# A fused attention and two-layer expert kernel: first-batch attention outputs copied to SBUF, and a new order of all steps

## The chip, the cores and the metric

The kernel runs on one core of a Trainium2 chip. The time is the device time of one execution in microseconds, the median of three runs. The engines are TensorE (PE; its weight loads are shown apart as PEld), VectorE (DVE), ScalarE (ACT), GpSimd (POOL) and SyncE (SP), which sends all the DMA transfers of this kernel from one queue, in order. Each engine works off its own instructions in order.

## The reference

Three stages follow each other; everything is float32, and the inputs of stage 2 and 3 have 1152 rows.

```python
# stage 1: attention, 2 batches x 8 heads x 576 positions x 64
rel = pos[:, None] - pos[None, :]
mask_plain = (rel >= 0) & (rel < 32)                    # heads 0 to 3
mask_dil = (rel >= 0) & (rel < 128) & (rel % 4 == 0)    # heads 4 to 7
scores = np.where(masks, (q @ k.T) / 8, -1e9)
attn = softmax(scores);  x = (attn @ v) -> 1152 x 512
# stage 2: w_in 512 x 1024, w_out 1024 x 512
h = x @ w_in
solu = h * softmax(h)
ln = (solu - mean) / sqrt(var + 1e-6) * g_ln
x = ln @ w_out
# stage 3: 4 experts, w1 512 x 1024, w2 1024 x 512 each
p = domain_probs / domain_probs.sum(-1)
out = sum over e of p[:, e] * (relu(x @ w1[e]) @ w2[e])
```

## The kernel before

Every matrix product outside the attention is computed from split operands: a value is held as a high part in a short form and a low part (value minus high part), and a product is three matmuls, high x high, high x low and low x high. `w_in` and `w_out` come as 64-bit floats and are rebuilt to float32 and split on the chip.

**Stage 1.** Per batch there are six units of attention: `UP.t.b` for the plain heads, `UD.t.b` for the dilated ones (t = 0 to 2, b the batch). A unit (`att_U`) starts with the masks (L264, L268) and the scores (L277) on PE into a PSUM tile `pa`, of which there are two buffers. DVE takes the maximum (L285) and subtracts it (L287); ACT does the exponential (L290); DVE sums (L292) and inverts (L294); the weights `pd` are multiplied on DVE or POOL (L296). PE transposes them (L315) into a `pa`, they are copied to `pt` (L170, L172), and PE multiplies with V (L326, the AV product) into another `pa`. The last two steps write the split output: the high part `xhi` by a copy from PSUM (ACT L172 or DVE L170), the low part `xlo` by `lo_psum` (L246), a subtraction on DVE of the high part in SBUF from the PSUM tile. Units in `ASWAP` are transposed by DVE and a round trip through DRAM instead (`sta`, `da`, L301 to L309).

**The weights.** `VI.j` rebuilds and splits block j of `w_in` (`VI.4` is the second half of block 0) in seven steps: two passes of ACT (L186, L188), a shift (L190) and a merge (L192) on DVE, an addition (L194), the high part `wh` (L170, L172), and the low part `wl` (L221). `VO.j.t` does that for `w_out` (`conv_out`, low part L237); its raw data is in `cvr`, of which there are two halves. `l...` are loads, by SyncE: `lP`, `lD` for the scores' inputs `qkP`, `qkD`, `lvp`, `lvd` for V, `lI` for `w_in` (`draw`), `lO` for `w_out`.

**Stage 2.** `H.t` (`moe_H`, L356) multiplies token tile t of 128 rows with `w_in`: four quarters, of six matmuls each, one for each block of `w_in`, then the reductions of the gated softmax and of the normalization. `T.t` transposes the result, on PE for tiles 0 to 2 and through DRAM for the others, and splits it into `hh` and `hl`. `X.c.dp` (`moe_X`, L432) multiplies chunk c of three token tiles with `w_out`.

**Stage 3.** Each expert's two layers, 512 x 1024 and 1024 x 512, are computed with seven products of quarter matrices in place of eight, `u` (L545) and `d` (L617). `XQ`, `WP` and `WV` prepare the sums of operands for it.

**What sets the order.** Everything up to the middle of the first expert is issued by the table `ORDER`, L27 to L50. Each step is a Python generator, and one name in the table runs it to its next `yield`. A `+` behind a name sets `alt[0]` for this step: a `copy` then runs on DVE instead of ACT (`copy`, L168), and a `pick()` on POOL instead of DVE (L162). `F.n` issues n matmuls on a constant tile whose output nobody reads. The table decides the order on every engine and in SyncE's queue, since nothing else reorders.

Of the kernel before, what the change touches and what calls it, by code (L numbers as in the profile page):

```python
# [26 lines left out]
ORDER = """  # L27
lP.0.0+ F.6 UP.0.0 UP.0.0+ lI.0 UP.0.0 lD.0.0 VI.0 VI.0 VI.0+ VI.0 F.6 UD.0.0 UP.0.0 UP.0.0+ lI.4 VI.0 VI.4+ UD.0.0 UP.0.0+ VI.4 UD.0.0+ UD.0.0+ lD.1.0+ VI.4
VI.4 VI.4+ lP.1.0+ F.3 UD.1.0 UD.1.0 UD.1.0+ UD.0.0 UD.0.0 UD.1.0+ UP.1.0 UP.1.0 UD.1.0 UD.1.0+ UP.0.0 VI.0 UP.1.0+ lD.2.0+ F.1 UD.2.0+ UD.2.0 lP.2.0 F.1
UP.2.0 UD.0.0+ UD.2.0 VI.4 UP.1.0+ UP.1.0+ lI.1+ UP.1.0+ VI.1+ VI.1+ UD.1.0+ lvd.1.0+ UP.2.0 UP.2.0+ UP.2.0 UD.1.0 VI.1+ VI.1 F.3 UP.0.0 UP.1.0 UD.1.0 VI.4+  # L30
F.1 UD.1.0+ UD.1.0+ UP.0.0 lI.2+ UD.1.0+ VI.0+ lvp.0.0+ UP.0.0 VI.2+ VI.2 UP.0.0 UP.0.0+ VI.1+ F.3 H.0+ VI.2 VI.2+ UD.2.0 VI.1 VI.1 UD.0.0 UD.0.0 UP.2.0+
UP.1.0 lI.3 UP.1.0 lvd.0.0 UD.0.0+ lvp.1.0 UP.1.0 lvp.2.0+ H.0+ UD.2.0+ VI.3 UD.0.0 UD.0.0 UP.1.0 UP.1.0 VI.3+ UD.2.0 VI.3 lP.0.1 UP.0.1 H.1 H.1 VI.2+ VI.2
UP.0.1 UP.0.1+ UP.0.1+ lO.0.0+ VO.0.0 VI.3 UD.2.0+ UD.2.0 UD.2.0 VI.3 VI.3 VI.3+ VI.2 lD.0.1+ UD.0.1 UD.0.1 UD.0.1+ lvp.0.1 lD.1.1+ UP.0.1 UP.2.0+ lvd.2.0+
UD.1.1 VO.0.0 lO.0.1 VO.0.1 UP.0.1 H.0 UD.1.1 VO.0.0 UD.2.0 UD.2.0 VO.0.0 VO.0.0+ H.0 UP.2.0+ lO.1.0+ lD.2.1 UD.2.0 H.0+ UD.0.1 UD.0.1+ endE+ UD.1.1+ VO.0.1+
VO.0.1+ H.0+ H.0 H.1 H.1 misc+ UP.0.1+ UP.0.1 UD.0.1+ UD.0.1+ H.1+ UP.2.0 UD.1.1 UD.0.1+ UD.0.1 UP.0.1 UP.0.1 UP.2.0 H.0+ UP.0.1 UP.0.1+ VO.0.1+ UD.1.1
lvd.1.1 UP.2.0 VO.0.1+ H.2 UP.2.0 lvd.0.1+ UP.2.0 UD.1.1 H.1+ H.1+ UD.1.1+ VO.0.0+ VO.0.0+ VO.0.1+ VO.0.1+ UD.2.1 UD.2.1+ VO.1.0+ VO.1.0 VO.1.0+ VO.1.0 lP.2.1
VO.1.0+ T.0 H.1+ lvp.2.1+ UD.2.1 lO.1.1+ UD.0.1+ T.0+ T.0 H.2+ UD.1.1+ UD.1.1+ H.2 UD.2.1+ UD.2.1+ T.0+ UD.2.1 UD.2.1+ T.1+ T.1 T.1 H.3 T.1 H.2 H.2 lP.1.1
VO.1.1+ VO.1.1 VO.1.1+ lO.2.0+ UD.0.1+ UD.0.1 UP.2.1+ UP.2.1+ UD.0.1+ VO.1.0 VO.1.0 VO.1.1 UD.1.1+ UP.2.1+ H.2+ UD.2.1+ UD.2.1 H.3 H.3 VO.2.0 VO.2.0 VO.1.1+
lO.2.1 UP.2.1 UD.1.1+ UP.2.1+ lvd.2.1 UD.1.1 T.2 VO.2.0+ UD.1.1+ H.4 T.2+ T.2 UD.2.1 VO.1.1+ UP.2.1 VO.2.0 VO.2.0+ lO.3.0+ T.2 H.3+ H.3+ UP.2.1+ UP.2.1 VO.1.1
H.4 UP.1.1 VO.2.1 VO.2.1 VO.2.1+ UP.2.1 UP.1.1 UP.2.1 VO.2.1+ VO.2.1+ lO.3.1 lvp.1.1 H.4+ H.4+ UP.1.1 H.3+ VO.2.0 VO.2.0 X.0.1 UP.1.1+ VO.3.0+ UP.1.1 UP.1.1+  # L40
UP.1.1 UP.1.1 UP.1.1+ X.0.0 VO.3.0+ VO.3.0 VO.2.1 VO.3.1 VO.2.1 VO.3.1 VO.3.0+ UD.2.1 VO.3.0 VO.3.0+ VO.3.1+ VO.3.1 VO.3.1 VO.3.1 VO.3.0+ VO.3.1 UP.1.1+
UD.2.1 UP.2.1+ UP.2.1+ X.0.1 UD.2.1 T.3+ T.3+ T.3 UP.1.1 H.4+ endA+ X.0.1+ T.4 T.3+ T.4 T.4+ X.0.0 X.0.0+ UP.1.1 UP.1.1 H.5 H.5 UP.2.1 H.5+ H.5+ H.5 H.5 T.4
T.5 T.5+ T.5+ T.5+ H.6+ H.6+ T.4+ T.3+ T.3+ H.6+ H.6+ H.6+ H.8 H.8+ T.6+ H.7+ T.6 H.8+ H.8 T.6+ T.6+ T.4+ H.8+ T.5+ T.5 H.7+ H.7+ T.8 H.7 H.7 T.8+ T.8+ X.1.1+
X.1.1 T.7+ T.7+ T.7 T.8 sc T.7+ T.6 T.6+ X.1.0 T.8 X.1.0+ T.8 X.1.1 T.7+ T.7 X.1.0 endH+ XQ.0 lW.0+ XQ.0 XQ.0 XQ.0 XQ.0+ WP.0 WP.0 WP.0 X.2.1 XQ.0 XQ.0 WP.0
XQ.0 XQ.0 XQ.0+ X.2.0+ WP.0 WP.0 WP.0 WP.0+ XQ.0 XQ.0 WP.0 WP.0+ WP.0 X.2.1+ WP.0 WP.0+ endX+ XQ.0 WP.0 WP.0+ XQ.0 XQ.0 WP.0+ WP.0 WP.0 XQ.0 X.2.0 XQ.1 XQ.1
XQ.1 XQ.1 u.0 u.0+ u.0+ u.0 u.0+ u.0 u.0+ u.0+ u.0+ XQ.1+ XQ.1 lW.2 u.0+ XQ.1 u.0 lV.0 u.0+ u.0 u.0+ u.0+ XQ.1 u.0+ XQ.1 u.0+ u.0 u.0+ u.0+ WV.0 WV.0 WV.0
WV.0 u.1 u.1 u.0+ u.0+ lW.1 u.1+ XQ.1 XQ.1+ XQ.1 u.0 XQ.1+ u.1+ WP.1+ u.1+ WP.1 u.0 WP.1+ d.0+ d.0 u.1+ u.1+ u.1+ u.1 u.1+ u.1+ u.1+ XQ.1 WP.1+ XQ.1+ u.1+
WP.1 WP.1+ d.2 WP.1 WP.1+ lV.1 d.2+ XQ.1 d.1 d.1+ u.1 u.1 u.1+ u.1 u.1+ u.1 u.1 d.3+ d.3+ WP.1 u.1+ u.1+ u.1+ WP.1 WP.1+ u.1+ WP.1+ WP.1 WP.1+ WP.1+ WP.1+
WP.1 WP.1
"""  # L50
# [736 lines left out]
```

## Time and profile before

| | |
|---|---|
| median of 3 runs | 524.12 us (523.95 to 524.27) |
| the profiled execution | 524.0 us, of which the trace spans 522.2 |
| granted clock of PE in the profiled execution | 1.000 |
| PE busy | 510.8 us (98%) |
| DVE, ACT, POOL busy | 353.8, 190.8, 186.5 us |
| scores and AV products of stage 1 | up to 83 us |
| matmuls of stage 2 (L356, L432) | 22.6 to 143 us |
| products of stage 3 | from 143.4 us |
| bytes by DMA | 46.44 MB, mean 89 GB/s |

PE is busy in nearly the whole span. A busy share of another engine says little by itself; what counts is where PE waits, and for whom. PE's idle time stands in the first 25 us, in short gaps up to 110 us, and in the last 3 us.

### The profile page before, as it was taken

What the parts mean: (1) busy time and instruction counts of PE and PEld (TensorE: products, weight loads), DVE (VectorE), ACT (ScalarE), POOL (GpSimd) and SP (SyncE); (2) the same over time, 40 slices, a digit from 0 to 9 for tenths busy, and PEclk for the clock granted to TensorE, in tenths of its full rate; (3) what the DMA queues carried; (4) which work ended last, traced back from release to release, by engine and by line L of the source; (5) the groups of instructions that cost most, each with busy time, mean ns of one, the idle gap of its engine ahead of it and who ended that gap; (6) DMA issues with size and microseconds to landing.
All of it is one profiled execution on the core that took longest, in us unless ns stands there. A gap on an engine that the chain in (4) does not pass through costs nothing.

```text
span 522.2 us, 9460 instructions
## 1 busy us (share of the span) xinstructions
PE 510.8 (98%) x3993; PEld 457.0 (88%) x3999; DVE 353.8 (68%) x475; ACT 190.8 (37%) x294; POOL 186.5 (36%) x130
## 2 busy tenths in 40 slices
PE   7799999999999999999999999999999999999997
...
GB/s 320 399 208 257 218 161 93 142 169 178 41 202 80 2 1 100 63 1 0 162 0 1 51 111 1 0 161 2 1 3 160 1 0 82 1 0 1 1 82 100
DMA packets 24634, 46.44 MB, mean 89 GB/s; under 512 B 4496, under 2 KB 9104, under 8 KB 24208
## 3 DMA queue, kind: packets, MB, share of 16 engines
q1 hardware_dynamic: 24592, 45.84, 26.0%
...
## 4 chain that ended last, share of the span: by engine, by line
PE 90%; DMA 5%; ACT 2%; DVE 1%; issue 1%; SPq 0%; ACTq 0%
PE pa L617 19%; PE pm L617 19%; PE pm L545 17%; PE pa L545 17%; PE pm L356 8%; PE pm L432 8%; DMA draw<-in_moe_w_in_dram 2%; PE pa L326 1%; DMA qkD<-in_qkd_dram 1%; DMA da<-sta 1%; DMA cvr<-in_moe_w_out_dram 1%; PE pa L387 1%; PE pa L277 1%; ACT e L363 0%; ACT cva L188 0%
## 5 line engine op out<-in xcount | busy, mean ns | idle before, releaser
L558 DVE SCALAR_TENSOR_TENSOR hl<-ct,hh 128x512 fp32r<-128x512 f32 (+1 forms) x64 | 63.0, 1002 | 34.0 <-ACT hh L556 34.0
L556 ACT ACTIVATE hh<-ct 128x512 fp32r<-128x512 f32 (+1 forms) x64 | 42.2, 682 | 54.7 <-DVE ct L588 24.3
L617 PE MATMUL pa<-wl,hh 128*128 128x512 f32 (+1 forms) x148 | 57.3, 387 | 0.0
L617 PE MATMUL pa<-wh,hh 128*128 128x512 f32 (+1 forms) x148 | 57.2, 387 | 0.0
L617 PE MATMUL pa<-wh,hl 128*128 128x512 f32 (+1 forms) x148 | 57.1, 386 | 0.0
L545 PE MATMUL pm<-xoh,hl 128*128 128x256 f32 (+1 forms) x192 | 56.8, 296 | 0.0
L545 PE MATMUL pa<-xoh,hl 128*128 128x256 f32 (+1 forms) x192 | 56.8, 296 | 0.0
L545 PE MATMUL pm<-xol,hh 128*128 128x256 f32 (+1 forms) x192 | 56.8, 296 | 0.0
L545 PE MATMUL pa<-xol,hh 128*128 128x256 f32 (+1 forms) x192 | 56.8, 296 | 0.0
L545 PE MATMUL pm<-xoh,hh 128*128 128x256 f32 (+1 forms) x192 | 56.8, 296 | 0.0
L545 PE MATMUL pa<-xoh,hh 128*128 128x256 f32 (+1 forms) x192 | 56.8, 296 | 0.0
L617 PE MATMUL pm<-wl,hh 128*128 128x512 f32 (+1 forms) x144 | 55.7, 387 | 0.0
L617 PE MATMUL pm<-wh,hh 128*128 128x512 f32 (+1 forms) x144 | 55.7, 387 | 0.0
L617 PE MATMUL pm<-wh,hl 128*128 128x512 f32 (+1 forms) x144 | 55.6, 386 | 0.0
L464 POOL TENSOR_TENSOR wl<-wl,wh 128x1024 fp32r<-128x1024 f32 x7 | 16.9, 2414 | 95.6 <-ACT wh L172 95.6
L464 POOL TENSOR_TENSOR hl<-sw,hh 128x512 fp32r<-128x512 f32 x23 | 34.3, 1495 | 42.6 <-ACT hh L172 24.7
L622 DVE SCALAR_TENSOR_TENSOR xf<-pm,pr,xf 128x512 f32<-128x512 f32 (+1 forms) x32 | 23.6, 738 | 31.1 <-PE pm L617 31.1
L622 DVE SCALAR_TENSOR_TENSOR xf<-pa,pr,xf 128x512 f32<-128x512 f32 (+1 forms) x32 | 23.6, 738 | 30.4 <-PE pa L617 30.4
L172 ACT CAST wh<-wl 128x1024 fp32r<-128x1024 f32 x16 | 16.7, 1052 | 71.0 <-PE pa L617 40.6
L545 PEld LDWEIGHTS pa<-xoh,hh 128*128 128x128 f32 x192 | 36.4, 190 | 0.4
L545 PEld LDWEIGHTS pa<-xol,hh 128*128 128x128 f32 x192 | 36.4, 190 | 0.3
L545 PEld LDWEIGHTS pm<-xoh,hh 128*128 128x128 f32 x192 | 36.4, 190 | 0.3
...
## 6 DMA issues: line engine op xcount, KB each, us to landing
...
```

What stands on the lines that cost most here:

```text
L172: nc.scalar.copy(out, in_)
L277: nc.tensor.matmul(ps[32 * g:32 * g + 32, j, 64 * m:64 * m + 64], lhsT=qt[rows, h, xq:xq + 32], rhs=kt[rows, h, xq:xq + 64], start=False, ...
L326: nc.tensor.matmul(po[64 * (g % 2):64 * (g % 2) + 64, j, o:o + 32], lhsT=vt[rows, m, g, :], rhs=pt[rows, m, g, :], start=True, stop=True)
L356: nc.tensor.matmul(pm[:, n, :], lhsT=xx[:, kk, cols], rhs=ww["in", kk][:, 512 * n:512 * n + 512], start=(n_ == 0 and i < 2), stop=(n_ == K ...
L387: nc.tensor.transpose(pa[:, f // 4, (f % 4) * 128:(f % 4) * 128 + 128], e[:, f // 4, (f % 4) * 128:(f % 4) * 128 + 128], ident)
L432: nc.tensor.matmul(pm[:, dd, 0:CW], lhsT=w_, rhs=x_[:, f, :], start=(f == 0 and i == 0), stop=(f == KF - 1 and i == 2))
L464: pick().tensor_tensor(out=out, in0=a, in1=b, op=op)
L545: nc.tensor.matmul(ps[:, ff, 0:n], lhsT=a[:, kk, fc], rhs=b[:, kk, :], start=kk == 0 and m == 0, stop=kk == 1 and m == 2)
L556: nc.scalar.activation(out=hv, in_=src, func=AF.Relu)
L558: nc.vector.scalar_tensor_tensor(out=lv, in0=src, scalar=0.0, in1=hv.bitcast(F32), op0=ALU.max, op1=ALU.subtract)
L617: nc.tensor.matmul(po[:, 0, 0:dn], lhsT=h_[:, f, cols], rhs=w_, start=(f == 0 and i == 0), stop=(f == 3 and i == 2))
L622: nc.vector.scalar_tensor_tensor(out=acc[:, t, dc], in0=po[:, 0, 0:dn], scalar=pr[:, t, e:e + 1], in1=acc[:, t, dc], op0=ALU.mult, op1=ALU ...
```

## The change

A set `LSET` names the six units of the first batch. For these, ACT copies the AV product from PSUM to a new SBUF tile `av` (two buffers) right after it; the high part is then copied from `av` and the low part is `av` minus the high part, a subtraction that runs on DVE or POOL by the step's `+`. The units of the second batch go on as before. The table `ORDER` is replaced as a whole; the unread matmuls (`F`) go from 24 to 31 in it. Lines behind the new ones are shifted by 8 in the kernel after (L356 is L364 there, L326 and before stay).

```diff
--- before.py
+++ after.py
@@ -22,31 +22,31 @@
 XCUT = (2, 2, 4)
 NEG = -8.0e9
 SWAP = (3, 4, 5, 6, 7, 8)
+LSET = ("UP.0.0", "UD.0.0", "UD.1.0", "UP.1.0", "UD.2.0", "UP.2.0",)
 ASWAP = ("UD.0.1", "UD.1.1", "UD.2.1", "UP.1.1", "UP.2.1")
 
 ORDER = """
-lP.0.0+ F.6 UP.0.0 UP.0.0+ lI.0 UP.0.0 lD.0.0 VI.0 VI.0 VI.0+ VI.0 F.6 UD.0.0 UP.0.0 UP.0.0+ lI.4 VI.0 VI.4+ UD.0.0 UP.0.0+ VI.4 UD.0.0+ UD.0.0+ lD.1.0+ VI.4
...
+lD.0.0+ F.5 UD.0.0+ lP.0.0+ UP.0.0 UD.0.0+ UD.0.0+ UD.0.0+ UD.0.0+ UD.0.0 lI.0+ VI.0 VI.0 UP.0.0+ UD.0.0+ lI.4+ UP.0.0 VI.0 VI.0 VI.4+ VI.4 lD.1.0 lP.1.0+
...
 """
 
 @with_exitstack
@@ -327,6 +327,11 @@
                                      start=True, stop=True)
         yield
         segs = []
+        own = f"U{quad}.{t}.{b}" in LSET
+        pf = po[:, :, 0:TH]
+        if own:
+            po = ap2.tile([128, 2, TH], F32, name="av", tag="av")
+            nc.scalar.copy(po, pf)
         if quad == "P":
             s0 = b * S + TH * t
             segs.append((xhi[:, 0:2, s0:s0 + TH], xlo[:, 0:2, s0:s0 + TH], po[:, :, 0:TH]))
@@ -343,7 +348,10 @@
             copy(hv, pv)
         yield
         for hv, lv, pv in segs:
-            lo_psum(lv, pv, hv)
+            if own:
+                pick().tensor_tensor(out=lv, in0=pv, in1=hv.bitcast(F32), op=ALU.subtract)
+            else:
+                lo_psum(lv, pv, hv)
 
     lns = {}
 
```

First, DVE in the start-up, where the second block of `w_in` (`draw1`, `eva`, `wh1`, `wl1`) is converted while the scores of UP.2.0 (the tile `sm2`) come in. Before:

```order
L285 TENSOR_REDUCE st_405<-pa_363 128x6
L287 TENSOR_TENSOR sm2_133<-pa_363,st_405 128x6x64
L190 TENSOR_SCALAR eva_400<-eva_400 128x1024
L192 SCALAR_TENSOR_TENSOR eva_400<-draw1_395,eva_400 128x1024
L296 TENSOR_TENSOR pd0_128<-sm0_131,st_323 128x2x3x64
L170 CAST xhi_93<-pa_427 128x2x2x48 x2
L246 TENSOR_TENSOR xlo_94<-pa_427,xhi_93 128x2x2x48 x2
L246 TENSOR_TENSOR xlo_94<-pa_463,xhi_93 128x2x192
L190 TENSOR_SCALAR cva_164<-cva_164 128x1024
L192 SCALAR_TENSOR_TENSOR cva_164<-draw2_456,cva_164 128x1024
L221 TENSOR_TENSOR wl1_399<-eva_400,wh1_398 128x1024
L292 TENSOR_REDUCE st_405<-sm2_133 128x6
```

and in the kernel after:

```order
L285 TENSOR_REDUCE st_410<-pa_381 128x6
L287 TENSOR_TENSOR sm2_133<-pa_381,st_410 128x6x64
L170 COPY pt_424<-pa_415 128x384
L190 TENSOR_SCALAR eva_422<-eva_422 128x1024
L192 SCALAR_TENSOR_TENSOR eva_422<-draw1_299,eva_422 128x1024
L194 ISA eva_422<-draw1_299,eva_422 128x2048
L170 CAST xhi_93<-av_467 128x2x2x48 x2
L292 TENSOR_REDUCE st_410<-sm2_133 128x6
L292 TENSOR_REDUCE st_369<-sm1_132 128x6
L352 TENSOR_TENSOR xlo_94<-av_503,xhi_93 128x2x192
L221 TENSOR_TENSOR wl1_421<-eva_422,wh1_420 128x1024
L294 RECIPROCAL st_369<-st_369 128x6
```

The conversion of block 2 (`cva`, `draw2`) and the low parts `xlo` from PSUM no longer stand ahead of `wl1`; a copy, the addition for block 1 (`eva` with `draw1`, L194) and one low part that reads `av` do.

Second, PE around the first tile of stage 2: `pm` is H.0's sum, `wh0`, `wl0` the first block of `w_in` and `wh1`, `wl1` the second, L315 the transposes and L326 the AV products of two units. Before:

```order
L356 MATMUL pm_498<-wh0_205,xhi_93 128x512 x2
L356 MATMUL pm_498<-wl0_206,xhi_93 128x512 x2
L356 MATMUL pm_498<-wh0_205,xlo_94 128x512 x2
L315 MATMUL pa_510<-ident_74,pd1_129 128x128 x3
L315 MATMUL pa_517<-ident_74,pd0_128 128x128 x3
L326 MATMUL pa_526<-pt_514,vd00_116 64x32 x24
L326 MATMUL pa_553<-pt_523,vp_551 64x32 x24
L356 MATMUL pm_498<-wh1_398,xhi_93 128x512 x2
L356 MATMUL pm_498<-wl1_399,xhi_93 128x512 x2
L356 MATMUL pm_498<-wh1_398,xlo_94 128x512 x2
```

and after:

```order
L315 MATMUL pa_507<-ident_74,pd1_129 128x128 x3
L315 MATMUL pa_524<-ident_74,pd0_128 128x128 x3
L364 MATMUL pm_538<-wh0_234,xhi_93 128x512 x2
L364 MATMUL pm_538<-wl0_235,xhi_93 128x512 x2
L364 MATMUL pm_538<-wh0_234,xlo_94 128x512 x2
L364 MATMUL pm_538<-wh1_420,xhi_93 128x512 x2
L364 MATMUL pm_538<-wl1_421,xhi_93 128x512 x2
L364 MATMUL pm_538<-wh1_420,xlo_94 128x512 x2
L326 MATMUL pa_551<-pt_511,vd00_116 64x32 x24
L326 MATMUL pa_579<-pt_531,vp_408 64x32 x24
```

The two quarters of H.0 now follow each other, with the transposes ahead of them and the two AV products behind.

Third, SyncE's queue at the start: the loads of the scores' inputs, the blocks of `w_in` and V. Before:

```order
L147 DMA qkD01_114<-in_qkd_dram 128x896
L147 DMA qkP01_111<-in_qkp_dram 128x832
L147 DMA qkD02_115<-in_qkd_dram 128x896
L147 DMA qkP02_112<-in_qkp_dram 128x832
L208 DMA draw1_395<-in_moe_w_in_dram 128x1024
L150 DMA vd01_117<-in_vd_dram 128x768
L208 DMA draw2_456<-in_moe_w_in_dram 128x1024
L155 DMA vp_461<-in_vp_dram 128x768
L208 DMA draw3_521<-in_moe_w_in_dram 128x1024
L150 DMA vd00_116<-in_vd_dram 128x768
```

and after:

```order
L147 DMA qkD01_114<-in_qkd_dram 128x896
L147 DMA qkP01_111<-in_qkp_dram 128x832
L147 DMA qkD02_115<-in_qkd_dram 128x896
L208 DMA draw1_299<-in_moe_w_in_dram 128x1024
L147 DMA qkP02_112<-in_qkp_dram 128x832
L150 DMA vd01_117<-in_vd_dram 128x768
L155 DMA vp_408<-in_vp_dram 128x768
L155 DMA vp_475<-in_vp_dram 128x768
L208 DMA draw2_516<-in_moe_w_in_dram 128x1024
L150 DMA vd00_116<-in_vd_dram 128x768
L208 DMA draw3_529<-in_moe_w_in_dram 128x1024
```

`qkP02` has gone behind `draw1`, and a second `vp` is ahead of `draw2`.

Last, SyncE's queue at the end of the `w_out` loads (`cvr`); `da10`, `da11` and `da9` are DRAM tiles of attention units of the second batch. Before:

```order
L309 DMA pt_1200<-da10_1111 64x4x96 x2
L224 DMA cvr_163<-in_moe_w_out_dram 128x512
L305 DMA da11_1253<-sta_1212 128x2x192
L309 DMA pt_1257<-da11_1253 64x4x96 x2
L224 DMA cvr_163<-in_moe_w_out_dram 128x512
L155 DMA vp_1263<-in_vp_dram 128x768
```

and after:

```order
L305 DMA da11_1229<-sta_1227 128x2x192
L309 DMA pt_1236<-da10_1187 64x4x96 x2
L224 DMA cvr_163<-in_moe_w_out_dram 128x512
L309 DMA pt_1344<-da11_1229 64x4x96 x2
L224 DMA cvr_163<-in_moe_w_out_dram 128x512
L305 DMA da9_1413<-sta_1310 128x2x192
```

The write to `da11` is ahead of the `pt` pair of `da10`, and the seventh load of `w_out` (the first `cvr` row in the piece after) is ahead of the `pt` pair of `da11`.

## Rows read from the trace of the kernel before

**Rows 1.** The page: busy time by engine, and PE's busy tenths in 40 slices.

```profile
PE 510.8 (98%) x3993; PEld 457.0 (88%) x3999; DVE 353.8 (68%) x475; ACT 190.8 (37%) x294; POOL 186.5 (36%) x130
...
PE   7799999999999999999999999999999999999997
```

**Rows 2.** The stretches: length, PE, PEld, DVE, ACT, POOL busy, PEclk, DMA, GB/s.

```profile
10.00:20.00 10.00, 6.35 (x229) 4.26 (x233) 9.20 (x20) 6.30 (x12) 5.58 (x5) 1.00 1.02 415
20.00:30.00 10.00, 9.22 (x243) 7.19 (x244) 9.65 (x17) 8.98 (x12) 6.89 (x3) 1.00 1.00 373
...
40.00:50.00 10.00, 9.76 (x191) 7.81 (x190) 9.97 (x21) 9.29 (x16) 3.63 (x5) 1.00 0.77 253
```

**Rows 3.** What PE waited for from 22 to 145 us: total, times, longest.

```profile
PE pm L432 <- DVE wl L237: 0.6, 1, 0.6
...
PE pm L432 <- DVE hl L419: 0.2, 1, 0.2
```

**Rows 4.** Timeline of PE, start-up: start, length, instruction, [idle before, releaser].

```profile
14.22 0.68 PE L277 MATMUL pa<-qkD 64*32 64x64 f32 x43 [0.94 <-issue]
...
15.82 0.72 PE L277 MATMUL pa<-qkP 64*32 64x64 f32 x48
...
22.57 0.72 PE L356 MATMUL pm<-wh,xhi 128*128 128x512 f32 x2
...
25.18 1.12 PE L326 MATMUL pa<-pt,vd 64*64 64x32 f32 x48 [0.30 <-ACT pt L172]
...
26.93 0.73 PE L356 MATMUL pm<-wh,xhi 128*128 128x512 f32 x2
...
28.42 0.34 PE L264 MATMUL pa<-mask,identb 128*128 128x192 bf16 x2
```

**Rows 5.** Timeline of DVE, start-up.

```profile
21.58 1.54 DVE L246 TENSOR_TENSOR xlo<-pa,xhi 128x192 fp32r<-128x192 f32 x3
23.03 0.77 DVE L190 TENSOR_SCALAR cva<-cva 128x1024 uint32<-128x1024 uint32 x1
...
24.98 1.22 DVE L221 TENSOR_TENSOR wl<-eva,wh 128x1024 fp32r<-128x1024 f32 x1
...
31.77 1.23 DVE L194 CUSTOM_DVE_ANT_0 eva<-draw,eva 128x2048 uint16<-128x2048 uint16 x1
```

**Rows 6.** Timeline of POOL, start-up.

```profile
13.49 0.83 POOL L296 TENSOR_TENSOR pd<-sm,st 128x384 f32<-128x384 f32 x1 [0.45 <-DVE st L294]
...
20.62 2.63 POOL L194 TENSOR_TENSOR eva<-eva,draw 128x1024 uint32<-128x1024 uint32 x1 [2.54 <-ACT pt L172]
25.29 3.21 POOL L194 TENSOR_TENSOR cva<-cva,draw 128x1024 uint32<-128x1024 uint32 x1 [2.05 <-ACT pt L172]
28.96 1.14 POOL L296 TENSOR_TENSOR pd<-sm,st 128x384 f32<-128x384 f32 x1 [0.45 <-DVE st L294]
```

**Rows 7.** Timeline of ACT, start-up.

```profile
16.32 1.16 ACT L186 ACTIVATE draw<-draw 128x1024 int32<-128x1024 uint32 x1 [0.20 <-DMA draw<-in_moe_w_in_dram]
...
19.93 1.17 ACT L186 ACTIVATE draw<-draw 128x1024 int32<-128x1024 uint32 x1 [0.28 <-DMA draw<-in_moe_w_in_dram]
...
32.78 0.48 ACT L172 COPY pt<-pa 128x384 f32<-128x384 f32 x1 [1.04 <-PE pa L315]
```

**Rows 8.** Timeline of DVE and POOL where they collide.

```profile
133.57 0.69 DVE L464 TENSOR_TENSOR ct<-xf 128x512 f32<-128x512 f32 x1
...
134.36 1.52 POOL L464 TENSOR_TENSOR hl<-sw,hh 128x512 fp32r<-128x512 f32 x1 [12.43 <-DVE ct L464]
...
134.64 1.79 DVE L464 TENSOR_TENSOR hl<-sw,hh 128x512 fp32r<-128x512 f32 x1
```

**Rows 9.** The chain of waits ahead of 80.6 us: start, length, what.

```profile
66.74 4.30 DMA da<-sta
...
72.45 4.26 DMA cvr<-in_moe_w_out_dram
...
79.87 0.67 DVE wl L237
```

More of the change, by code (lines that the diff above doesn't have):

```diff
@@ L24 @@
 SWAP = (3, 4, 5, 6, 7, 8)
+LSET = ("UP.0.0", "UD.0.0", "UD.1.0", "UP.1.0", "UD.2.0", "UP.2.0",)
 ASWAP = ("UD.0.1", "UD.1.1", "UD.2.1", "UP.1.1", "UP.2.1")
 ORDER = """
-lP.0.0+ F.6 UP.0.0 UP.0.0+ lI.0 UP.0.0 lD.0.0 VI.0 VI.0 VI.0+ VI.0 F.6 UD.0.0 UP.0.0 UP.0.0+ lI.4 VI.0 VI.4+ UD.0.0 UP.0.0+ VI.4 UD.0.0+ UD.0.0+ lD.1.0+ VI.4
-VI.4 VI.4+ lP.1.0+ F.3 UD.1.0 UD.1.0 UD.1.0+ UD.0.0 UD.0.0 UD.1.0+ UP.1.0 UP.1.0 UD.1.0 UD.1.0+ UP.0.0 VI.0 UP.1.0+ lD.2.0+ F.1 UD.2.0+ UD.2.0 lP.2.0 F.1
-UP.2.0 UD.0.0+ UD.2.0 VI.4 UP.1.0+ UP.1.0+ lI.1+ UP.1.0+ VI.1+ VI.1+ UD.1.0+ lvd.1.0+ UP.2.0 UP.2.0+ UP.2.0 UD.1.0 VI.1+ VI.1 F.3 UP.0.0 UP.1.0 UD.1.0 VI.4+
@@ L31 @@
[L31 to L46, printed above, removed]
@@ L47 @@
-WV.0 u.1 u.1 u.0+ u.0+ lW.1 u.1+ XQ.1 XQ.1+ XQ.1 u.0 XQ.1+ u.1+ WP.1+ u.1+ WP.1 u.0 WP.1+ d.0+ d.0 u.1+ u.1+ u.1+ u.1 u.1+ u.1+ u.1+ XQ.1 WP.1+ XQ.1+ u.1+
-WP.1 WP.1+ d.2 WP.1 WP.1+ lV.1 d.2+ XQ.1 d.1 d.1+ u.1 u.1 u.1+ u.1 u.1+ u.1 u.1 d.3+ d.3+ WP.1 u.1+ u.1+ u.1+ WP.1 WP.1+ u.1+ WP.1+ WP.1 WP.1+ WP.1+ WP.1+
-WP.1 WP.1
+lD.0.0+ F.5 UD.0.0+ lP.0.0+ UP.0.0 UD.0.0+ UD.0.0+ UD.0.0+ UD.0.0+ UD.0.0 lI.0+ VI.0 VI.0 UP.0.0+ UD.0.0+ lI.4+ UP.0.0 VI.0 VI.0 VI.4+ VI.4 lD.1.0 lP.1.0+
+VI.4 VI.4+ VI.4+ UP.0.0+ UP.0.0 F.7 UD.1.0+ UD.1.0 lD.2.0 UD.1.0+ UD.1.0+ UP.0.0+ VI.0 UD.1.0 UP.0.0+ VI.4 VI.4+ lI.1+ lP.2.0+ F.3 UP.1.0 UP.1.0+ UD.1.0+
```

19 lines of the change are left out of this document (added).

## The prediction

> **What bounds the kernel now.** I read the page's busy shares first. TensorE (PE) works 510.8 us of the span of 522.2, and only the first and the last of its 40 slices show a 7 where the others show 9 [rows 1]. So whatever the change does for other engines is worth at most the 11.4 us in which PE stands still. The table by stretches says where those are: 3.65 us between 10 and 20 us, 0.78 in the next 10, 0.24 from 40 to 50, at a granted clock of 1.00 throughout [rows 2]. Then the waits of PE from 22 us to 145 us, of which the two that stage 2 and the expert operands own are 0.6 us for a low part of w_out (`wl`, L237) and 0.2 us for `hl` [rows 3]. Behind 145 us the chain of waits is PE after PE up to the tail, so the expert stages can lose but hardly win.
>
> Two further readings matter. In the stretch from 10 to 30 us VectorE (DVE) is the fuller engine (9.20 and 9.65 of 10 us against PE's 6.35 and 9.22) [rows 2]: there PE follows DVE. And the stretch ends in PE's first matmul of stage 2 at 22.57, whose second quarter, with `wl1`, starts at 26.93 [rows 4]; `wl1` is written by DVE from 24.98 for 1.22 us, to 26.20 [rows 5]. From there on PE has a backlog, and time is lost only if an input is late.
>
> The profiled run took 524.0 us, of which 1.8 lie outside its span; the median of three is 524.12. I sum on 524.0 and add the 0.1 at the end, where it is under the 0.2% (1.05 us) that I count as no change.
>
> **The change part by part.** Named sizes first. Six copies by ScalarE (ACT) of 128x384 from PSUM at 0.48 each, by a `pt` copy of that shape, are 2.9 us [rows 7]. ACT is busy 6.30 us between 10 and 20 us and 8.98 in the next 10 [rows 2]: a single copy can be hidden, but in the second of these there is 1 us to spare and about two copies fall there. Uncovered, a copy costs its 0.48. Five of the six low parts go to GpSimd (POOL) and one stays on DVE. The trace shows no POOL subtraction of that shape in the first batch's place; the nearest rows are its `pd` products of 128x384 at 0.83 to 1.14 [rows 6], so 4.2 to 5.7 us together; I take 5, with the end that collisions reach. DVE had 1.54 for three [rows 5]. In exchange the new order gives the additions of the second and third w_in block (2.63 and 3.21 on POOL [rows 6]) to DVE at 1.23 each, by the custom addition at 31.77 [rows 5].
>
> *DVE up to `wl1`.* By the two orders, in front of `wl1` DVE loses three low parts (1.54 together) and the shift and merge of the third block (1.95, from 23.03 to the next row's 24.98), 3.5 us [rows 5]; `pd` products that go against sums that come, all over 128x384 from SBUF. It gains one `pt` copy (about 0.5, by ACT's 0.48 [rows 7]), the custom addition (1.23 [rows 5]) and one low part from SBUF (0.5, as from PSUM): 2.2 us. Net -1.3. Against it: the loads stand in another order. `qkP02` (416 KB) goes behind the second w_in block, and a group of 6 unread matmuls stands before its scores. The second and third blocks land at 16.3 and 19.9, the start of ACT's first pass over each [rows 7]; 384 + 1024 KB lie between (by the loads' shapes in the order), so 390 KB/us. Hence the block now lands 1.1 us earlier (15.2), `qkP02` at 16.3 instead of 13.7, and the third block at about 21.9, two `vp` loads being ahead of it. The scores of UP.2.0 start at 15.82 before [rows 4] and now at 16.9 or later. DVE is in order, their maximum and subtraction stand ahead of the conversion, so it waits about 0.8. Net: `wl1` done at 25.7 instead of 26.2, between 25.0 and 26.6; the upper end is the 0.94 issue gap of [rows 4] falling on UP.2.0's scores.
>
> *PE from there.* In the new order H.0's first two quarters stand together, ahead of the two AV products that stood between them. Before, both were done at 28.42 with the products, which start at 25.18 and leave at 26.93 [rows 4]. The same work now: second quarter from about 25.9, 1.5 us; the products 1.75; hence 28.2 to 29.2, and centre 28.4. DVE then has 10.8 us of instructions up to `wl3`, by its order's rows and this trace's durations, so H.0 and H.1 come to their ends at the same place as before (within 0.1 by my replay, which follows both engines row by row). Seven more unread matmuls fall before 22 us, none longer than a matmul of H.0 over as many columns (0.72 for two [rows 4]), 2.5 us at most, where PE stands idle for 3.65 us in the second 10 us alone [rows 2]: hidden, except that each stands ahead of something. I put the start as a whole at +0.1, between -0.7 and +0.9.
>
> *The gap at 80.6.* PE waits 0.6 there for `wl` of the last w_out block [rows 3]. The chain is read backwards: the low part at 79.87, the block's load from 72.45, and, ahead of it in SyncE's queue, the pair of `pt` loads that had waited for the DRAM write `da` from 66.74 for 4.30 [rows 9]. That queue is in order. In the new one `da11` is written ahead of another `pt` pair, and the seventh w_out load goes ahead of the `pt` pair that reads it; only the eighth stands behind. By replay the eighth is sent some 0.8 earlier, of the 1.4 between the write's landing and 72.45. Of the 0.6 that PE lost I take back 0.5, between 0 and 0.6. Against it, the `hl` of T.2 is later in DVE's row, so that X.0 can stall at its start: +0.15, between 0 and 0.3, the 0.2 of [rows 3] being its nearest relative.
>
> *The gap at 41.* The 0.24 from 40 to 50 us [rows 2] lies behind two groups of transposes whose `pt` copies both follow at once. In the new order one group goes up between H.1's quarters, so one of the two products finds its tile: -0.12, between 0 and -0.24.
>
> *X.2 to the first expert.* ACT now casts two blocks of second-layer weights ahead of copies that the first products read. The trace of before shows nothing of the kind; 0 to 0.5 (half a block's cast), and I take 0.1, since PE has X.2 to work on.
>
> From 160 us on the instructions are the same: 0. Sum: 0.1 - 0.5 + 0.15 - 0.12 + 0.1 = -0.27 on 524.0, 523.7; with the 0.1 to the median **523.8**. Its own range, from the terms' ends taken together in part, is 522.9 to 524.9.
>
> **What speaks against the change.** Two instructions that read SBUF can hold each other up. At 134.36 POOL starts a subtraction and at 134.64 DVE starts one of 128x512, which takes 1.79 us where its neighbour took 0.69 [rows 8]. It goes the other way too: DVE starts `wl1` at 24.98, POOL its addition at 25.29, and DVE's 1.22 is undisturbed while POOL takes 3.21 instead of 2.63 [rows 5, 6]. So the one that started first keeps its pace, at 1.1 us for DVE when it is second. Before, the low parts read PSUM and SBUF on DVE; now five POOL reads of SBUF lie between DVE's conversions. On the other hand POOL's two long additions (5.8 us) leave the same stretch, and these are longer than what comes (about 5). I count it as even in the sum, and as a rival below.
> [...]
>
> **The rivals.**
> 1. *Relief of DVE carries (faster), 0.30.* `wl1` at 25.0, PSUM buffers free after ACT's copy rather than after the subtraction, the start shorter by 0.7, the gaps at 41 and 80.6 gone (0.24 + 0.6): 524.0 - 1.5 = 522.5. For it: DVE at 9.2 to 9.65 of 10 [rows 2]. Against: the 1.1 us by which UP.2.0's scores come later.
> 2. *The start gets longer (slower), 0.22.* One mechanism: UP.2.0's scores, behind 1 MB of w_in and 6 unread matmuls, hold DVE's in-order queue while the second block, already through ACT, waits behind them. It decides from `wl1` starting later than 25.2, that is ending after 26.4, a little behind the trace of before. With the 0.94 gap on the scores `wl1` ends at 26.6 and H.0 waits 0.9 us; a POOL read in DVE's way on `wl2` (1.1) is the same queue once more, but H.1 has 0.5 of slack by then. 524.0 + 0.9 + 0.4 (half of X.0's and the first expert's upper ends) = 525.3. For it: the load sizes. Against: net 1.3 us less in front of `wl1`.
> 3. *Collisions of DVE behind POOL (slower), 0.04.* Two of them, on `wl1` and `wl3`, at 1.1 each [rows 8], with the gap at 80.6 taken back (-0.5): 524.0 + 2.2 - 0.5 = 525.7. Against: POOL works less there than before.
> 4. *Nothing moves at all: 524.0, with the likeliest case.* The order's pieces cancel and the last w_out block stays late because its load waits for something else.
>
> **How the numbers follow.** The forecast has 0.40 and rival 4 0.04, nearly all of it within 0.2% of 524.12, that is from 523.07 to 525.17, with 0.04 below by the forecast's lower edge; rival 1 has 0.30, a tenth of it within; rivals 2 and 3 have 0.26, about 0.03 of it within. So faster 0.27 + 0.04 = 0.31, same 0.46, slower 0.23. The range 522.2 to 525.5 holds both sides' middles and leaves about 1 in 10 beyond each end.
>
> **What would show it.** Right: `wl1` written before 26.0; H.0's first two quarters together; H.1 ended at 41 +- 0.5; the wait for `wl` L237 at 80 us under 0.3; and the stages from 160 us to the end as long as before. Wrong on the slow side: UP.2.0's scores after 17.5 with DVE idle behind them, or DVE rows of 1024 elements at 2 us and more beside POOL's low parts. Wrong on the fast side: the first matmul of H.0 before 22 and PE idle under 3 us between 10 and 20. A stall at the first expert above 0.5 us would break the last term.

## The result, and the profile after

The kernel after took 528.27 us, the median of 22 runs (527.20 to 531.96), against 525.59 us for the kernel before (22 runs, 522.87 to 528.76): a ratio of 1.0056 (95% interval 1.0039 to 1.0073). Forecast were 523.8 us, in a range of 522.2 to 525.5, from the 524.12 of the three runs of the kernel before known then. The profiled execution of the kernel after took 527.65 us with a span of 525.9, 3.7 more than before. That of the kernel before (524.0) is one of its faster ones: by the medians the loss is 2.7 us.

The page of the kernel after, busy times, slices and DMA queues (kind: packets, MB, share of 16 engines):

```profile
PE 512.5 (97%) x4000; PEld 458.0 (87%) x4006; DVE 354.6 (67%) x468; ACT 194.7 (37%) x303; POOL 187.2 (36%) x134
...
PE   6879999999999999999999999999999999999997
...
PEclk9989999999999999999999999999999999999999
...
q1 hardware_dynamic: 24592, 45.84, 25.8%
q8 instruction: 31, 0.51, 0.4%
```

Against [rows 1], PE is busy 1.7 us more and idle 2.0 us more (13.4 against 11.4). The loss is early: the fourth digit of PE is 9 and the third 7, and PEclk shows an 8 there, where before all were 9. The stretches say the same (columns as in [rows 2]). The kernel before from 30 to 40 us:

```profile
30.00:40.00 10.00, 10.00 (x196) 8.04 (x195) 9.79 (x17) 5.93 (x10) 4.67 (x5) 1.00 0.37 132
```

and the kernel after:

```profile
10.00:20.00 10.00, 7.58 (x221) 4.86 (x225) 8.92 (x20) 5.23 (x10) 6.52 (x6) 1.00 1.03 411
20.00:30.00 10.00, 9.21 (x268) 6.65 (x269) 9.66 (x14) 9.04 (x15) 1.92 (x3) 1.00 1.03 401
30.00:40.00 10.00, 7.03 (x171) 5.51 (x169) 6.81 (x10) 5.44 (x9) 2.23 (x3) 0.83 0.75 288
40.00:50.00 10.00, 10.00 (x190) 8.16 (x188) 8.67 (x17) 7.55 (x15) 6.86 (x7) 1.00 0.17 53
```

From 10 to 30 us PE does no less than in [rows 2], and DVE is as full. Between 30 and 40 us PE works 7.03 us, where it worked throughout before (10.00), and the granted clock's mean is 0.83. What PE waited for from 22 to 170 us:

```profile
PE pa L268 <- issue: 3.0, 1, 3.0
PE pa L268 <- ACT av L334: 0.3, 1, 0.3
PE pa L326 <- DVE hl L246: 0.3, 1, 0.3
PE pm L440 <- DVE hl L427: 0.2, 1, 0.2
```

The wait for `wl` of [rows 3] is gone. In its place stand 2.97 us ahead of a mask matmul, put down to "issue": the engine waited for nothing that the profile shows. The timeline of PE around it:

```profile
16.73 0.72 PE L277 MATMUL pa<-qkP 64*32 64x64 f32 x48 [0.57 <-DMA qkP<-in_qkp_dram]
...
23.16 0.74 PE L364 MATMUL pm<-wh,xhi 128*128 128x512 f32 x2
...
28.43 0.33 PE L264 MATMUL pa<-mask,identb 128*128 128x192 bf16 x2
...
29.73 0.27 PE L268 MATMUL pa<-mask,identb 64*32 64x192 bf16 x6 [0.33 <-ACT av L334]
32.97 0.26 PE L268 MATMUL pa<-mask,identb 64*32 64x192 bf16 x2 [2.97 <-issue]
...
33.76 1.22 PE L364 MATMUL pm<-wh,xhi 128*128 128x512 f32 x2
...
36.86 0.71 PE L364 MATMUL pm<-wh,xhi 128*128 128x512 f32 x2
...
46.53 1.60 PE L326 MATMUL pa<-pt,vp 64*64 64x32 f32 x96
```

At 28.43 both kernels are at the same instruction at the same time (28.42 in [rows 4]). Then six of eight mask matmuls of a unit run, and PE stops in the middle of them. The first pair of L364 matmuls behind the gap takes 1.22 us where the later one at 36.86 takes 0.71: from 33.32 to 36.73 us the granted clock is 0.50, as the stretch shows:

```profile
33.32:36.73 3.41, 3.41 (x43) 2.56 (x26) 2.79 (x4) 0.94 (x2) 0.00 (x0) 0.50 1.04 403
```

PE works 3.41 us there at a granted clock of 0.50 and so loses some 1.7 (an estimate from these two numbers). The next point that both kernels share is the double AV product at 46.53. Before:

```profile
41.88 1.60 PE L326 MATMUL pa<-pt,vp 64*64 64x32 f32 x96 [0.24 <-ACT pt L172]
```

The loss there is 4.65 us, and 2.97 + 1.70 is 4.67. From there on the kernel after gains 1.0 back (the `wl` wait of 0.6 among it): 3.7 in the span.

DVE answers to [rows 5] with

```profile
23.49 0.92 DVE L352 TENSOR_TENSOR xlo<-av,xhi 128x384 fp32r<-128x384 f32 x1
24.46 1.23 DVE L221 TENSOR_TENSOR wl<-eva,wh 128x1024 fp32r<-128x1024 f32 x1
...
30.32 0.56 DVE L287 TENSOR_TENSOR sm<-pa,st 128x384 f32<-128x384 f32 x1
33.87 0.56 DVE L285 TENSOR_REDUCE st<-pa 128x6 f32<-128x384 f32 x1 [2.98 <-PE pa L277]
```

`wl1` ends at 25.69; behind the gap DVE stands 2.98 us, since its next scores come from PE.

### The profile page after: what moved, and what is told of

Its sections match the earlier page's. It is cut to its first block, busy times and chain, and to the rows that moved or that the text cites. A ratio compares the mean times of both kernels' runs of the same rounds, so it can differ in the third digit from the quotient of the medians.

```text
span 525.9 us, 9481 instructions
## 1 busy us (share of the span) xinstructions
PE 512.5 (97%) x4000; PEld 458.0 (87%) x4006; DVE 354.6 (67%) x468; ACT 194.7 (37%) x303; POOL 187.2 (36%) x134
## 4 chain that ended last, share of the span: by engine, by line
PE 90%; ACT 4%; DMA 2%; issue 1%; DVE 1%; SPq 1%; ACTq 0%; DVEq 0%
PE pa L625 19%; PE pm L625 18%; PE pm L553 17%; PE pa L553 17%; PE pm L440 10%; PE pm L364 7%; DMA qkP<-in_qkp_dram 2%; PE pa L326 1%; PE pa L277 0%; ACT e L371 0%; ACT e L376 0%; SPq L147 0%; ACT draw L186 0%; ACT av L334 0%; ACT e L397 0%
## 5 line engine op out<-in xcount | busy, mean ns | idle before, releaser
L472 POOL TENSOR_TENSOR wl<-wl,wh 128x1024 fp32r<-128x1024 f32 x7 | 16.9, 2414 | 95.2 <-ACT wh L172 95.2
L472 POOL TENSOR_TENSOR hl<-sw,hh 128x512 fp32r<-128x512 f32 x21 | 31.5, 1498 | 38.0 <-ACT hh L172 28.0
L172 ACT CAST wh<-wl 128x1024 fp32r<-128x1024 f32 x16 | 16.9, 1054 | 70.9 <-PE pa L625 40.4
L580 POOL TENSOR_TENSOR ct<-ct,ct 128x512 f32<-128x512 f32 (+1 forms) x15 | 22.2, 1481 | 50.3 <-ACT ct L578 50.3
L553 PEld LDWEIGHTS pm<-xol,hh 128*128 128x128 f32 x192 | 36.4, 190 | 0.3
```

The source lines that it names most:

```text
L172: nc.scalar.copy(out, in_)
L472: pick().tensor_tensor(out=out, in0=a, in1=b, op=op)
L553: nc.tensor.matmul(ps[:, ff, 0:n], lhsT=a[:, kk, fc], rhs=b[:, kk, :], start=kk == 0 and m == 0, stop=kk == 1 and m == 2)
L580: poolv().tensor_tensor(out=c12, in0=c21, in1=c22, op=ALU.add)
```

## The experiments

What can stop an engine that waits for no semaphore? The page has a second kind of DMA traffic, "instruction": 31 transfers on queue 8, 16 KB each and 0.51 MB in all. PE has 4000 + 4006 instructions, 258 for each of the 31. So queue 8 seems to bring PE's instructions, in blocks of 256, which makes 64 bytes each (an inference from these counts, and from the gaps 256 apart below). One such transfer lies in the gap, from 30.58 to 31.70. The queues from 30.5 to 31.75 us:

```profile
q1 hardware_dynamic: 145, 0.45, 96.8%
q8 instruction: 1, 0.02, 5.6%
```

Theory I: PE runs out of instructions, because the next block comes through DMA engines that are full of data (queue 1 takes 101.3% of their time from 22 to 36 us; 80.9% before). Rival A: the copies to SBUF and GpSimd's low parts starve PE. Rival B: some other wait that the new order brings. Rival C: PE needs something there that the profile doesn't show. Each expectation is quoted as it was written ahead of the run. "Issue" gaps are PE's.

**One load moved, after.** SyncE's order only; `lvp.0.1` waits for a buffer until 28 us and holds back what stands behind it.

```diff
- ... lvp.2.0 UD.2.0+ misc+ lD.1.1+ ... VO.0.1 lvp.0.1 UP.0.1+
+ ... lvp.2.0 lvp.0.1 UD.2.0+ misc+ lD.1.1+ ... VO.0.1 UP.0.1+
```

> The kernel after with one load moved: the fifth load of plain V (lvp.0.1), which waits for a buffer until about 28 us, stands right behind the fourth, so that the five loads behind it (qkD11, two w_out blocks, qkP12, vd10) are sent at 28 us and not at 23 to 28. Theory I (PE runs out of instructions: its next 16 KB come through the same DMA engines and lie behind the data loads; the clock then falls to half for 3.4 us): PE's gap of 2.97 us at 30 us, put down to issue, is gone or under 0.5, the clock 1.00 throughout, span 521.0 to 522.0, ratio to before 0.995 to 0.999. Rival A (the copies to SBUF and the low parts on GpSimd starve PE): gap and ratio stay, 1.005 to 1.007. Rival B (the new order itself makes later work wait): the gap may go, but the ratio stays over 1.003.

Measured: 1.0007 (0.9989 to 1.0026), 525.58 us. PE's timeline:

```profile
31.50 0.27 PE L268 MATMUL pa<-mask,identb 64*32 64x192 bf16 x6 [0.31 <-ACT av L334]
32.00 0.26 PE L268 MATMUL pa<-mask,identb 64*32 64x192 bf16 x2 [0.23 <-issue]
```

The gap at the same two instructions is 0.23 us. PE has the same instructions in the same order, so the 0.5% hang on what SyncE sends when. Rival A expected the gap to stay and rival B a ratio over 1.003: neither fits. It isn't one profile alone: the granted clock of the whole run is 0.987 to 0.997 in all 22 runs of the kernel after and 1.000 in 8 of the 12 here.

The ratio is outside theory I's 0.995 to 0.999, and the span (523.8) outside its 521.0 to 522.0. In the profiles, the stretch from the mask matmul of 28.43 in the kernel after (30.21 here) to the double AV product takes 14.13 us against 18.10, and 13.46 before, so most of the loss does come back. This run is late at its start: PE waits 3.5 us for `qkD01` (1.9 in the kernel after) and then runs 3.41 us at a granted clock of 0.50, from 12.22 on. Whether that also holds up the median of the twelve runs is not shown. The DMA engines between 29.7 and 30.7 us, where the block now comes, with next to no data:

```profile
q8 instruction: 1, 0.02, 6.0%
q1 hardware_dynamic: 1, 0.00, 0.1%
```

**The copies of one unit only, after.**

```diff
-LSET = ("UP.0.0", "UD.0.0", "UD.1.0", "UP.1.0", "UD.2.0", "UP.2.0",)
+LSET = ("UP.2.0",)
```

> The kernel after with its order, but LSET holds UP.2.0 alone: five units write their high part from PSUM again, and their low part by DVE from PSUM. Theory I: PE's instructions and the loads are the same, so the gap at 30 us stays at 2.5 to 3.5 us and the clock falls behind it; ratio 1.004 to 1.008. Rival A (copies): the gap goes, and the ratio falls under 1.002. Rival B: as theory I, without a gap put down to issue.

Measured: 1.0203 (1.0174 to 1.0233). All expectations fell. PE's waits in the first 60 us:

```profile
PE pa L315 <- DVE st L294: 2.8, 1, 2.8
PE pa L268 <- DVE sm L287: 2.5, 1, 2.5
...
PE pa L315 <- DVE xlo L246: 2.0, 1, 2.0
...
PE pa L264 <- DVE xlo L246: 1.2, 1, 1.2
```

The new order is made for the copies. With the low parts back on DVE, PE waits 8.5 us for DVE, some of it for a PSUM buffer that `xlo` still reads; with PE that late no block is missing (the block of the gap lasts 5.9 us there). So this run doesn't test theory I, but it refutes rival A: inside this order the copies save far more than they cost.

**All copies, order of before.**

```diff
 LSET = ("UP.0.0", "UD.0.0", "UD.1.0", "UP.1.0", "UD.2.0", "UP.2.0",)
-ORDER = """ (the table of after)
+ORDER = """ (the table of before)
```

> The order of before with the copies: LSET of all six units, the low parts on DVE or GpSimd by the old table's marks. Theory I: no gap of more than 0.5 us put down to issue near 30 us, since loads and PE's instructions are those of before; ratio 0.999 to 1.003. Rival A (copies): 1.004 or more, with waits of PE for av, xhi or xlo. Rival B: 1.000.

Measured: 1.0202 (1.0184 to 1.0221), outside theory I's 0.999 to 1.003, and inside rival A's number. PE's waits in the first 60 us:

```profile
PE pa L327 <- ACT pt L173: 2.8, 4, 1.3
...
PE pm L365 <- ACT xhi L173: 1.8, 1, 1.8
```

PE waits 4.6 us for `pt` and `xhi` from ACT, and the granted clock is 0.58 and 0.56 in the two stretches from 20 to 40 us. ACT in turn stands 3.90 us for GpSimd's `eva`, ahead of which the low parts of two units now stand in GpSimd's row (the second is shown); the first fence is ACT's, the second GpSimd's:

```profile
30.97 1.04 ACT L173 CAST wh<-eva 128x1024 fp32r<-128x1024 f32 x1 [3.90 <-POOL eva L195]
31.92 0.85 ACT L173 COPY pt<-pa 128x384 f32<-128x384 f32 x2
```

```profile
26.72 1.86 POOL L353 TENSOR_TENSOR xlo<-av,xhi 128x384 fp32r<-128x384 f32 x1 [2.14 <-ACT xhi L173]
28.55 2.39 POOL L195 TENSOR_TENSOR eva<-eva,draw 128x1024 uint32<-128x1024 uint32 x1
```

There is no "issue" gap of theory I's size. So the copies are not free by themselves: they are paid where the order doesn't make room for them. In the kernel after, all that PE waits for `av` is 0.3 us.

**More data in the queue, before.** SyncE's order only, the other way.

```diff
- ... UD.0.1+ lvp.0.1 lD.1.1+ ... VO.0.0 lO.0.1 VO.0.1 ...
+ ... UD.0.1+ lD.1.1+ ... VO.0.0 lO.0.1 lvp.0.1 VO.0.1 ...
```

> The kernel before with one load moved the other way: lvp.0.1, which waits for a buffer until 27 us, stands behind qkD11, vd02 and a w_out block (1.3 MB), so that these are sent at 23.6 us and not at 27.4. All engines but SyncE have the same instructions in the same order. Theory I: PE's fetch at 28.6 us, which ended only 0.4 us ahead of need, comes late: PE stands 1 to 3 us near 30 us, put down to issue, the clock falls behind it; ratio 1.002 to 1.009. Rivals A and B: nothing in it concerns copies or the new order, and the inputs come earlier: 0.998 to 1.001.

Measured: 0.9993 (0.9972 to 1.0015). In the profiled run the data take 100.6% of the DMA engines from 29.0 to 33.4 us, and the fetch starts 3.36 us after PE enters the block, as late as in the kernel after; but this block lasts 6.60 us, and the fetch lands 2.2 ahead of its end. Theory I as it stood was wrong: a full queue alone doesn't stop PE. The block's length had been left out. The "0.4 us ahead of need" of the expectation was a misreading as well: by the count below, the kernel before needed that block 3.0 us after it had landed.

**Six unread matmuls fewer, after.**

```diff
- ... UP.1.0 UP.1.0 UP.1.0 F.6 UP.2.0 lvp.1.0+ ...
+ ... UP.1.0 UP.1.0 UP.1.0 UP.2.0 lvp.1.0+ ...
```

> The kernel after without the 6 unread matmuls ahead of UP.2.0's scores: 12 PE instructions fewer (each matmul has its weight load) in front of everything behind, in a place where PE waits for a load anyway. The loads are those of after. Theory I (the next 16 KB of instructions are late): the block's border lies at a fixed number of instructions, so the gap of some 3 us stays but opens 12 instructions later in the program: not between the sixth and the seventh mask matmul (L268) of the fourth unit of scores but behind its second mask pair more and about four of its score matmuls (L277), with 44 behind the gap. Rival C (PE waits there for something that those mask matmuls need, which the profile doesn't show): the gap stays between the sixth and the seventh mask matmul, or goes.

One run, 528.77 us. PE's timeline:

```profile
30.66 0.28 PE L268 MATMUL pa<-mask,identb 64*32 64x192 bf16 x8 [0.32 <-ACT av L334]
30.74 0.30 PE L277 MATMUL pa<-qkD 64*32 64x64 f32 x4
33.93 0.68 PE L277 MATMUL pa<-qkD 64*32 64x64 f32 x44 [2.90 <-issue]
```

The gap is as long (2.90) and opens behind all eight mask matmuls and four score matmuls, with 44 behind it: 12 instructions later in the program, to the instruction. Rival C is out. The border is one of a count of instructions, not of anything that the instructions there need.

**The block's length.** I counted PE's instructions in each trace (matmuls, weight loads and the sequencer's own) in order of their start, with a border every 256. The spacing shows in the gaps: in the version with both loads moved (below) two gaps stand at 1211 and 1467 of the count, 256 apart:

```profile
29.62 0.26 PE L268 MATMUL pa<-mask,identb 64*32 64x192 bf16 x2 [0.55 <-issue]
...
35.39 0.67 PE L277 MATMUL pa<-qkD 64*32 64x64 f32 x42 [0.58 <-issue]
```

The table has the block that ends at instruction 1211 (1214 before), where the gap of the kernel after is; the fetch is queue 8's transfer from the DMA records. Times are us.

| kernel | PE enters the block | it is through after | fetch of the next one starts, after entry | lands | PE goes on, after landing | stands (start to start) |
|---|---|---|---|---|---|---|
| before | 25.94 | 6.48 | 2.68 | 29.59 | (in time) | 0.20 |
| after | 27.23 | 2.52 | 3.36 | 31.70 | 1.28 | 3.22 |
| first experiment | 29.01 | 2.51 | 0.73 | 30.70 | 1.30 | 0.48 |

By these rows the next block seems to be asked for when PE enters the present one (inferred: the traces show when the transfer starts, not when it is asked for, and among the long matmuls from 84 us on it starts up to 5.0 us ahead of PE's entry in the kernel before, and up to 4.8 in the kernel after, by this count). With idle DMA engines (the first experiment) the transfer starts 0.73 us after the entry, with full ones (the kernel after) 3.36; it takes 1.0 to 1.1, and PE goes on 1.3 after it has landed: a round of 3.0 us or of 5.8. In the kernel after PE is through with its block in 2.52 us and stands for the rest of the round: 3.36 + 1.11 + 1.28 - 2.52 = 3.23, measured 3.22. In the kernel before, H.0's second quarter (26.93 in [rows 4]) and H.1's first two lie between the two AV products and the later scores, and this block lasts 6.48 us:

```profile
29.34 0.73 PE L356 MATMUL pm<-wh,xhi 128*128 128x512 f32 x2
...
30.84 0.61 PE L356 MATMUL pm<-wh,xhi 128*128 128x512 f32 x2
```

In the new order the products, masks and scores follow each other, 256 short instructions in 2.5 us. In these runs a gap of 3 us took both: the short block (the first experiment has it too, beside idle engines, and stands 0.23) and the full queue (the kernel before with more data has it, with a long block, and doesn't stand).

**Still more data in the queue, after.**

```diff
- ... lvp.2.0 UD.2.0+ misc+ lD.1.1+ lO.0.0+ lP.2.1+ lO.0.1 VI.3 ...
+ ... UD.2.0+ misc+ lD.1.1+ lO.0.0+ lP.2.1+ lO.0.1 lvp.2.0 VI.3 ...
```

> The kernel after with its fourth load of plain V (lvp.2.0), which waits for a buffer until 22 us, moved behind two w_out blocks, so that five loads (2 MB) behind it are sent from 18 us on. Theory I: more data stand ahead of PE's instructions from 18 to 30 us, so PE's time put down to issue in the first 36 us grows from 3.5 us to 4 to 7, in one gap near 30 us or in a second one near 25 us; ratio 1.006 to 1.012. If the queue doesn't matter: one gap as before, 1.0056, or none, since the inputs come earlier.

Measured: 1.0057 (1.0034 to 1.0081), the same gap, 2.97 us. The queue was full already: the fetch starts 3.34 us after entry, as in the kernel after. "Grows" was wrong.

**An AV product first, after.** On PE alone; every other engine has the order of after.

```diff
- ... VI.2+ H.0 H.0 UD.0.0 UD.0.0 UP.1.0+ ...
+ ... VI.2+ UD.0.0 H.0 H.0 UD.0.0 UP.1.0+ ...
```

> The kernel after with one step moved on PE alone: UD.0.0's AV product stands ahead of H.0's first two quarters and not behind them; the loads, and every other engine's instructions, are those of after. Theory I, made sharper by the runs so far: the next 16 KB of instructions are asked for when PE enters a block of 256, and take 3.35 us (full DMA engines) + 1.1 + 1.3 us until PE goes on, 5.75 us in all; in the kernel after that block holds short matmuls only and is through in 2.5 us, so PE stands 3.2. Here both quarters of H.0 (3.2 us) come into the same block, which lasts some 5.4 us: gap of 0 to 0.7 us instead of 2.97, with the loads as full as before; ratio 1.000 to 1.003. If only the loads decide: the gap stays at 2.5 to 3.5, ratio 1.005 to 1.008.

Measured: 1.0021 (0.9999 to 1.0044). PE's timeline:

```profile
23.65 0.77 PE L326 MATMUL pa<-pt,vd 64*64 64x32 f32 x37 [0.31 <-ACT pt L172]
25.95 0.42 PE L326 MATMUL pa<-pt,vd 64*64 64x32 f32 x11 [1.52 <-issue]
...
32.52 0.72 PE L277 MATMUL pa<-qkD 64*32 64x64 f32 x48
```

With the loads as full as ever, the gap at the old border is gone, as forecast. A new one of 1.52 us, which I had not forecast, stands one border earlier: the block ahead lost H.0's two quarters and is through in 3.9 us, and its fetch landed only at 24.58. PE's last start ahead of it is at 24.21, 3.93 us after the entry at 20.28; the transfer started 3.24 after the entry and took 1.06, and PE went on 1.37 after the landing: 5.67 - 3.93 = 1.74, which is the time from start to start. A third one, of 0.30 us, stands one border behind the old one, at 38.00.

**Versions that beat both?** `qkP02` sent ahead of the second w_in block, as in the kernel before, on top of the first experiment (against the kernel after; the later `lvp.0.1` goes here too):

```diff
- ... lI.1+ lP.2.0+ F.3 ... lvp.2.0 UD.2.0+ ...
+ ... lP.2.0+ lI.1+ F.3 ... lvp.2.0 lvp.0.1 UD.2.0+ ...
```

> The version of the first experiment (lvp.0.1 early, no gap at 30 us), with qkP02 sent ahead of the second w_in block as in the kernel before. By the account so far DVE's idle 0.68 us ahead of UP.2.0's maximum (17.50 in the kernel after) goes, and wl1 comes up to 0.6 us earlier; ratio 0.998 to 1.001 to before, 0.5 us under the first experiment. If the load order at the start doesn't matter, the same 1.0007 as there.

Measured: 0.9987 (0.9965 to 1.0010), 525.02 us. Its interval overlaps that of the first experiment. With the AV product first as well:

> The same move on PE in the version with both loads moved (lvp.0.1 early, qkP02 ahead of the second w_in block), which ran at 0.9987 and still had gaps of 0.55 and 0.58 put down to issue at 29 and 35 us. Theory I: the first of these goes, the second stays or goes with the shifted block; ratio 0.996 to 0.999. If the move has a price of its own (PE waits 0.4 us for the pt tile ahead of the product): 0.999 to 1.001.

Measured: 1.0000 (0.9974 to 1.0026), with a gap of 1.57 us at the earlier border again, which the expectation missed; its ratio is outside 0.996 to 0.999. With the product between H.0's two quarters, and both loads still moved:

```diff
- ... VI.2+ H.0 H.0 UD.0.0 UD.0.0 UP.1.0+ ...
+ ... VI.2+ H.0 UD.0.0 H.0 UD.0.0 UP.1.0+ ...
```

> Both loads moved, and UD.0.0's AV product between the first and the second quarter of H.0. Theory I with its round of 3.0 us (idle DMA engines) to 6.4 us (full): the block up to PE's instruction 955 loses one quarter and lasts some 5.7 us, against a round of up to 6.4, so 0 to 0.7 us are lost there; the block behind it holds one quarter and lasts 4.0 us, against a round of 3.2, so the 0.55 of the version with both loads goes. Ratio 0.997 to 1.000. If the blocks don't decide: as that version, 0.9987, with its gaps in the same places.

Measured: 0.9984 (0.9964 to 1.0003), 524.40 us; the one gap of this kind on PE between 22 and 36 us is

```profile
28.20 0.47 PE L326 MATMUL pa<-pt,vd 64*64 64x32 f32 x17 [0.19 <-issue]
```

The block that ends there lasts 5.4 us against a round of 5.8 (3.32 + 1.12 + 1.39); the one behind it lasts 3.6, and its fetch lands 1.4 ahead of its end. And the kernel after once more, on that chip:

> The kernel after itself, unchanged, on the chip of the run beside it. Theory I: the gap of 2.9 to 3.0 us put down to issue at 29 to 31 us is there again, PE's clock falls behind it, and every run is over 526.5 us; ratio 1.004 to 1.008. If the first result was that of a chip or an hour: within 0.2% of before.

Measured: 1.0062 (1.0037 to 1.0086), 528.40 us:

```profile
33.25 0.31 PE L268 MATMUL pa<-mask,identb 64*32 64x192 bf16 x2 [3.10 <-issue]
```

So the last version is 4.0 us under the kernel after. Against the kernel before its interval still touches 1: no clear gain.

## Why the prediction was wrong

- *What bounds.* Right: PE, with DVE ahead of it up to 27 us; PE's 11.4 idle us became 13.4. The granted clock was taken as 1.00 throughout, and by the estimate above 1.7 us of the loss came through it (3.41 us at 0.50).
- *DVE up to `wl1`.* Forecast to end at 25.7, measured 25.69. UP.2.0's scores were forecast for 16.9 and came at 16.73. Two sizes were off: the low part from SBUF took 0.92 on DVE, not 0.5, beside a GpSimd low part that had begun at 22.64 and took 1.36 for two (by my estimate a collision as in [rows 8], at 0.4); and DVE's idle 0.68 at 17.5 was a little less than the 0.8 put in. Together they add 0.3 us, which something else in DVE's row must have given back, so the match to the tenth is partly luck.
- *PE from there.* This step failed, in the words "H.0 and H.1 come to their ends at the same place as before". Up to 28.43 the replay holds (28.4 was forecast); then PE stands 2.97 and works 3.41 us at half clock. The start as a whole was put at +0.1, at most +0.9, and measured +4.65 at the shared point. Without the two, the point shared by both kernels would be at 41.86 against 41.88. The replay counted what each instruction waits for and not how its code arrives: a block of 256 instructions through in 2.5 us, with the next one 5.8 us away.
- The trace of before already held a sign of the cause. The 0.94 of "issue" in [rows 4] stands at instruction 446 of the count above, three times 256 ahead of 1214, and a transfer of queue 8 landed at 12.66, 1.56 ahead of PE's next start: that block was through in 5.08 us against a round of 6.23 (3.68 + 0.99 + 1.56). I read that row as a gap that might fall on some scores, gave it 0.9 us in the slow rival, and did not ask what it was.
- *The gap at 80.6.* Right: gone (forecast -0.5, measured -0.6). *The gap at 41.* Gone; 0.3 for another AV product stands later. *X.0's stall and the first expert.* 0.15 and 0.1 were forecast; no such wait appears. The products of stage 3 begin at 147.0 against 143.4, 3.6 later, and the rest takes as long: right.
- *The rivals.* Slower had a chance of 0.23. The slow rival had the sign and the wrong mechanism: UP.2.0's scores didn't hold `wl1`, and none of the signs named for the slow side appeared. Collisions of DVE with GpSimd were small (the 0.4 by my estimate): GpSimd's low parts of five units, six instructions of 0.70 to 1.39, took 6.0 us in all, a little over the forecast's 4.2 to 5.7. No engine waits for one of them; PE's weight loads wait 0.5 us for DVE's own low part, the 0.92. The subtraction in question took 0.92 from two SBUF inputs beside GpSimd; from PSUM, rows of its shape in the kernel after took 0.54 and 0.88 beside GpSimd (at 50.5 and 63.6 us), and 0.55 to 0.84 without it (84.9 to 91.0 us). Whether the move to SBUF made the difference isn't shown by these rows. The range ended at 525.5, because no term had a bound for a stall without a cause in the program.
- *Open.* Runs of the kernel before lie between 522.9 and 530.4. The traces show PE's wait for `qkD01` in the first 12 us between 0.5 and 4.4 us from run to run; what sets it wasn't tried.
